# A second layer by 20 block products in place of 21: a 2x4 by 4x3 block algorithm with its sums spread over GpSimd, DMA and VectorE

## The chip, the cores and the metric

The kernel runs on one core of a Trainium2 chip. The metric is the device time of one execution in microseconds (us); the kernel before was run three times. TensorE multiplies matrices and writes PSUM (8 banks of 128 partitions x 512 float32), ScalarE and VectorE read and write PSUM and SBUF, GpSimd works on SBUF, and DMA moves data; each engine works through its own list of instructions in order and waits on semaphores. In the profile PE is TensorE, PEld its weight loads, DVE VectorE, ACT ScalarE, POOL GpSimd, and SP the engine that issues most of the DMA transfers.

## The reference

A causal convolution with 7 taps per head, and on its result a layer pair with a hard swish between, all in float32:

```python
x_unf = x_pad[:, idx, :].reshape(B, S, K, H, group)     # B, S, D = 8, 4096, 192; K = 7, H = 8
x = np.einsum('hk,bskhg->bshg', softmax(weight), x_unf).reshape(B * S, D)
h = x @ w_in                                             # 192 -> 2048
g = h * np.clip(h + 3.0, 0.0, 6.0) / 6.0
out = g @ w_out                                          # 2048 -> 192
```

## The kernel before

The 32768 tokens are worked through in 32 blocks of 1024 tokens. A block has two halves of 512 tokens, numbered k, and a stage each for the two layers. In the first stage (`h_phase`, unchanged) the first layer is computed into PSUM by a Strassen scheme, and `relu` (ScalarE) and `gate` (VectorE) make `g` from it, in four units of dff (the 2048 wide dimension); the second stage multiplies `g` by `w_out`. VectorE also convolves the tokens of the next block during the second stage: seven taps over 128x1536 elements, the first with one tensor as input, the other six with two.

```python
N, P = 512, 128                        # tokens of a half, partitions
g = cst.tile([P, NP, 2, G, N], F32)    # 8 chunks of dff, 2 halves of dff, 2 halves of tokens
def tap(part, k, t):                   # one tap of the convolution
    if k == 0:
        nc.vector.tensor_scalar(out=to, in0=x[...], scalar1=c, scalar2=None, op0=ALU.mult)
    else:
        nc.vector.scalar_tensor_tensor(out=to, in0=x[...], scalar=c, in1=to,
                                       op0=ALU.mult, op1=ALU.add)
def swap(part):                        # the other half's rows beside one's own, by two DMAs
    nc.sync.dma_start(out=y[D2:P, to], in_=y[0:D2, part])
    nc.sync.dma_start(out=y[0:D2, to], in_=y[D2:P, part])
def gate(out, r6, h):                  # h in PSUM, r6 and out in SBUF
    nc.vector.scalar_tensor_tensor(out=out, in0=r6, scalar=1.0, in1=h, op0=ALU.min, op1=ALU.mult)
```

Second stage before: Strassen's seven products of 2x2 blocks. A product is 512 tokens x 1024 of dff x 96 results, so 3 x 8 matmuls of a 128x32 weight tile with 512 tokens; four such tiles lie side by side in the array and run together (`side_by_side`). Of the sums of `g`, two are on GpSimd, unit by unit as `g` appears (`h_phase` calls them), and two on VectorE in the second stage. Each product is drained from PSUM to SBUF by a copy or an addition.

```python
def g_sums(engine, which, slots, width):
    forms = {1: (S1, A21, A22, ALU.add), 3: (S3, A11, A21, ALU.subtract),
             2: (S2, S1, A11, ALU.subtract), 4: (S4, A12, S2, ALU.subtract)}
    ...
            engine.tensor_tensor(out=o[:, r], in0=a[:, r], in1=b[:, r], op=op)
# h_phase, after each unit u > 0:
    g_sums(nc.gpsimd, (1, 3), range(2 * u - 2, 2 * u), 2)     # two of 128x1024

def out_strassen(i, conv):
    for u in conv:                     # the seven taps for block i + 1
        u()
    b, bank = three(1, 2, 0)           # product 1 and a third of product 2: 32 matmuls
    nc.scalar.copy(out=p1[:], in_=bank[m]); piece(p2, 0, bank, NQ); give(b)
    g_sums(nc.vector, (2,), every, 4)  # two of 128x2048
    b, bank = three(4, 2, 1)
    ...
    swap(slice(0, K3))
    b, bank = by_quarters(2, 2)
    ...
    g_sums(nc.vector, (4,), every, 4)
    ...                                # products 7, 6, 3, additions, three stores
    return [lambda: store(i, u3, 1, 1)]    # the fourth store: in the next h_phase

def out_last(i):                       # block 31: the last products in two halves of 256 tokens
    ...
```

The sums of weights are made once, on GpSimd, at the start: four of 128x768 for `w_out`, then four of 128x512 for `w_in` (`w_in_t`). Block 0 is multiplied without such sums (`out_direct`).

Of the kernel before, what the change touches and what calls it, by code (L numbers as in the profile page):

```python
# [16 lines left out]
def kernel(  # L17
# [7 lines left out]
):  # L25

# [96 lines left out]
    w_out = cst.tile([P, NP, 8, DH], F32, name="w_out")  # L123
    B11, B12, B21, B22, T1, T2, T3, T4 = range(8)
# [84 lines left out]
    def w_out_unit(j):  # L209
        dst = w_out[:, j, B11 : B22 + 1].rearrange("p b d -> p (b d)")  # L210
        return Rounding(lambda: load_w_out(j), dst)

    def w_sums():

        def sub(out, x, y):
            nc.gpsimd.tensor_tensor(out=out, in0=x, in1=y, op=ALU.subtract)

        for o, x, y in ((T1, B12, B11), (T3, B22, B12), (T2, B22, T1), (T4, T2, B21)):
            sub(w_out[:, :, o], w_out[:, :, x], w_out[:, :, y])
        b11, b12, b21, b22 = (w_in[:, c::2, s] for s in range(2) for c in range(2))  # L220
        t1, t2, t3, t4 = (w_in_t[:, j] for j in range(4))
        for o, x, y in ((t1, b12, b11), (t3, b22, b12), (t2, b22, t1), (t4, b21, t2)):
            sub(o, x, y)
# [63 lines left out]

    g = cst.tile([P, NP, 2, G, N], F32, name="g")
    g4 = g[:].rearrange("p c h k n -> p c (h k) n")
    A11, A21, A12, A22 = (g4[:, :, j] for j in range(4))  # L290
    S2, S3, S4 = A11, A21, A12
# [123 lines left out]
    def h_phase(left):  # L415
        work = {(u, k): Unit(u, k) for u in range(UNITS) for k in range(2)}
        for u, plan in enumerate(PLANS):
            for step in plan:
                if step == "X":
                    while left:  # L420
                        left.pop(0)()
                    continue
                op = step[1:].rstrip("'+")
                at = u + (step[-1] == "+") - (step[-1] == "'")
                if at < UNITS:
                    work[at, "LU".index(step[0])].run(op)
            if u:
                g_sums(nc.gpsimd, (1, 3), range(2 * u - 2, 2 * u), 2)
# [4 lines left out]
    def mm(bank, j, x, w, q, ps_, first, last, tokens=slice(0, N)):  # L433
# [4 lines left out]
                out=bank[j * QS : (j + 1) * QS, tokens], lhsT=w_out[:, p, w, cols],  # L438
                rhs=x[:, p, tokens],
# [13 lines left out]
    def store_rows(i, k, q, xt, j, dma=nc.sync, tokens=slice(0, N)):  # L453

        t0 = i * TB + k * N
        dma.dma_start(
            out=out[t0 + tokens.start : t0 + tokens.stop, q * QS : (q + 1) * QS].rearrange("(t r) d -> r t d", r=QS),
            in_=xt[j * QS : (j + 1) * QS, tokens].rearrange("r (t d) -> r t d", d=QS),
# [29 lines left out]
    def g_sums(engine, which, slots, width):  # L488

        forms = {  # L490
            1: (S1, A21, A22, ALU.add), 3: (S3, A11, A21, ALU.subtract),
            2: (S2, S1, A11, ALU.subtract), 4: (S4, A12, S2, ALU.subtract),
        }
        for n in which:
            o, a, b, op = forms[n]
            for p in slots[::width]:
                r = slice(p, p + width)
                engine.tensor_tensor(out=o[:, r], in0=a[:, r], in1=b[:, r], op=op)  # L498


    prod = {
        1: (A11, B11), 2: (A12, B21), 3: (S4, B22), 4: (A22, T4),
        5: (None, T1), 6: (S2, T2), 7: (S3, T3),
    }

    def product(bank, j, n, q, ks=every, **tokens):
        x, w = prod[n]
        return mm(bank, j, S1 if n == 5 else x, w, q, ks, True, True, **tokens)

    def four(*parts):  # L510

        b = take()
        bank = psum[:, b]
        side_by_side(*[product(bank, j, n, q) for j, (n, q) in enumerate(parts)])
        return b, bank

    def three(n, n4, q4):
        return four(*[(n, q) for q in range(NQ)], (n4, q4))

    def by_quarters(n, q):  # L520

        b = take()
        bank = psum[:, b]
        w = NP // 4
        side_by_side(
            *[product(bank, j, n, q, range(j * w, (j + 1) * w)) for j in range(4)]
        )
        return b, bank

    def rows(q):  # L530
        return slice(q * QS, (q + 1) * QS)

    def piece(dst, q, src, j):
        nc.scalar.copy(out=dst[rows(q)], in_=src[rows(j)])  # L534

    def pieces(dst, q, src):
        piece(dst, q, src, 0)
        for j in range(1, 4):
            add(dst[rows(q)], dst[rows(q)], src[rows(j)])
# [4 lines left out]
    def store(i, c, k, half_, qs=range(NQ), queues=(nc.sync,), tokens=slice(0, N)):  # L544

        xt = ot.tile([P, N], F32, name="xt")
        r = slice(qs[0] * QS, (qs[-1] + 1) * QS)
        nc.vector.transpose(out=xt[r, tokens], in_=c[r, tokens])  # L548
        for q in qs:
            store_rows(i, k, half_ * NQ + q, xt, q, queues[q % len(queues)], tokens)  # L550

    def sums_tiles():
        return (cs.tile([DH, N], F32, name=f"c{k}") for k in range(6))

    m = slice(0, DH)

    def out_last(i):

        both = nc.sync, nc.scalar
        p1, p2, p4, p5, u2, u3 = sums_tiles()  # L560
        b, bank = three(1, 2, 0)
        nc.scalar.copy(out=p1[:], in_=bank[m])
        piece(p2, 0, bank, NQ)
        give(b)
        g_sums(nc.vector, (2,), every, 4)
        b, bank = four((2, 1), (2, 2), (4, 0), (4, 1))
        for dst, q, j in ((p2, 1, 0), (p2, 2, 1), (p4, 0, 2), (p4, 1, 3)):
            piece(dst, q, bank, j)
        give(b)
        g_sums(nc.vector, (4,), every, 4)  # L570
        add(p2[:], p1[:], p2[:])
        store(i, p2, 0, 0)
        b7, bank7 = three(7, 5, 0)
        piece(p5, 0, bank7, NQ)
        b, bank = three(6, 5, 1)
        piece(p5, 1, bank, NQ)
        add(u2[:], p1[:], bank[m])
        give(b)
        add(u3[:], u2[:], bank7[m])
        give(b7)  # L580
        two = slice(0, 2 * QS)
        add(p4[two], u3[two], p4[two], ALU.subtract)
        store(i, p4, 1, 0, range(2))
        b, bank = by_quarters(5, 2)
        pieces(p5, 2, bank)
        give(b)
        add(u2[:], u2[:], p5[:])
        add(p5[:], u3[:], p5[:])
        store(i, p5, 1, 1)
        for t in range(0, N, N // 2):  # L590
            b = take()
            bank = psum[:, b]
            ts = slice(t, t + N // 2)
            side_by_side(*[
                product(bank, j, n, q, tokens=ts)
                for j, (n, q) in enumerate([(3, 0), (3, 1), (3, 2), (4, 2)])
            ])
            add(u2[:, ts], u2[:, ts], bank[m, ts])
            store(i, u2, 0, 1, queues=both, tokens=ts)
            add(u3[rows(2), ts], u3[rows(2), ts], bank[rows(NQ), ts], ALU.subtract)  # L600
            store(i, u3, 1, 0, range(2, 3), queues=both[::-1], tokens=ts)
            give(b)

    def out_strassen(i, conv):
        p1, p2, p4, p5, u2, u3 = sums_tiles()
        for u in conv:
            u()
        b, bank = three(1, 2, 0)
        nc.scalar.copy(out=p1[:], in_=bank[m])  # L609
        piece(p2, 0, bank, NQ)  # L610
        give(b)
        g_sums(nc.vector, (2,), every, 4)
        b, bank = three(4, 2, 1)
        nc.scalar.copy(out=p4[:], in_=bank[m])  # L614
        piece(p2, 1, bank, NQ)
        give(b)
        swap(slice(0, K3))
        b, bank = by_quarters(2, 2)
        pieces(p2, 2, bank)
        give(b)  # L620
        g_sums(nc.vector, (4,), every, 4)
        add(p2[:], p1[:], p2[:])
        store(i, p2, 0, 0)
        b7, bank7 = three(7, 5, 0)
        piece(p5, 0, bank7, NQ)
        y_sums()
        b, bank = three(6, 5, 1)
        piece(p5, 1, bank, NQ)
        add(u2[:], p1[:], bank[m])
        give(b)  # L630
        add(u3[:], u2[:], bank7[m])
        give(b7)
        add(p4[:], u3[:], p4[:], ALU.subtract)
        store(i, p4, 1, 0)
        b, bank = three(3, 5, 2)
        piece(p5, 2, bank, NQ)
        add(u2[:], u2[:], bank[m])
        give(b)
        add(u2[:], u2[:], p5[:])
        store(i, u2, 0, 1)  # L640
        add(u3[:], u3[:], p5[:])
        return [lambda: store(i, u3, 1, 1)]
# [18 lines left out]
    with tc.manual_schedule():  # L661
# [124 lines left out]
        S1 = ss.tile([P, NP, N], F32, name="s1")[:]  # L786
        left = []
        for i in range(1, NB):
            h_phase(left)
            if i + 1 < NB:  # L790
                left = out_strassen(i, conv_units(i + 1, [slice(0, K3)]))
            else:
                out_last(i)
            if i + 2 < NB:
                x_tiles[i + 2] = load_x(i + 2)

# [32 lines left out]
```

## Time and profile before

| | |
|---|---|
| time, median of 3 (lowest to highest) | 2410.32 us (2410.22 to 2411.18) |
| span of the profiled execution | 2408.5 us, 40221 instructions |
| granted TensorE clock | 1.000 |
| second stage, one steady block | 36.19 us |
| first stage, one steady block | 38.08 us |

Reading: the page's part 1 gives each engine's busy time as a share of the span; part 4 follows the chain of work that ended last back from the end; the groups give every kind of instruction with its count, its mean duration and the idle time before it; the timeline lists instructions by start and duration, with neighbours of one kind merged (x6 is six of them, the duration is that of all six). A group's mean can mix instructions that ran alone with ones that had to wait while running, so the timeline of one block is read beside it. The program's matmul of float32 appears as two records.

### The profile page before, as it was taken

To read this page: it belongs to the slowest core of one execution; us is meant where nothing else is said; L and a number is where in the kernel's file an instruction comes from. 1 tells how busy PE (TensorE), PEld (TensorE's weight loads), DVE (VectorE), ACT (ScalarE), POOL (GpSimd) and SP (SyncE) were. 2 spreads that over 40 slices of the span, in tenths; PEclk is the share of its full clock that TensorE was granted. 3 is DMA by queue.
4 is the path that set the end of the run, shared out by engine and by line. 5 is a ranking of instruction groups with operands and counts; after the bars stand their busy time and mean duration, and the time that the engine had idled before them with its cause. 6 is when DMAs were issued, how large, how long until landed. Compare 5 with 4: busy or idle time off the path is not lost.

```text
span 2408.5 us, 40221 instructions
## 1 busy us (share of the span) xinstructions
PE 2400.5 (100%) x16536; PEld 1019.8 (42%) x16536; DVE 2089.4 (87%) x2533; ACT 1078.4 (45%) x1828; POOL 672.2 (28%) x280
## 2 busy tenths in 40 slices
PE   9999999999999999999999999999999999999999
PEld 5434444334444344443444434444344444344443
DVE  8788888988888888898888898888898888888896
ACT  7234553345543355433454334553345543355433
POOL 2423321233221333122332223322233312333122
PEclk9999999999999999999999999999999999999999
DMA  5211122101222011221112211122201122111210
GB/s 145 40 26 29 27 40 40 39 19 25 39 41 40 19 36 27 40 41 22 33 27 40 41 33 22 27 40 40 40 18 31 34 40 41 21 34 27 40 27 14
DMA packets 227400, 84.65 MB, mean 35 GB/s; under 512 B 205520, under 2 KB 210640, under 8 KB 227216
## 3 DMA queue, kind: packets, MB, share of 16 engines
q1 hardware_dynamic: 225880, 81.56, 17.2%
q8 instruction: 129, 2.11, 0.4%
q10 hardware_dynamic: 1240, 0.27, 0.1%
q14 instruction: 55, 0.45, 0.1%
q0 software_dynamic: 96, 0.26, 0.0%
HBM read 31.72 MB, written 25.17 MB: 24 GB/s over the span
## 4 chain that ended last, share of the span: by engine, by line
PE 99%; DVE 1%; DMA 0%; issue 0%; ACTq 0%; ACT 0%; DVEq 0%
PE psum L311 51%; PE psum L437 48%; DVE c L542 0%; DMA x<-in_x_dram 0%; DVE y L263 0%; DMA out_dram<-xt 0%; DVE xt L548 0%; DVE top L178 0%; ACTq L92 0%; PE psum L676 0%; DVE scale L174 0%; DVE y L259 0%; ACT c L534 0%; DVE scale L195 0%; DVEq L548 0%
## 5 line engine op out<-in xcount | busy, mean ns | idle before, releaser
L437 PE MATMUL psum<-g,w_out 128*32 128x512 f32 (+1 forms) x9376 | 1163.7, 590 | 0.0
L311 PE MATMUL psum<-y,w_in 64*128 64x512 f32 x3664 | 885.2, 591 | 0.6 <-POOL w_in L203 0.3
L498 POOL TENSOR_TENSOR s<-g 128x1024 f32<-128x1024 f32 x124 | 293.6, 2367 | 1644.5 <-DVE g L321 1644.5
L317 ACT ACTIVATE r<-psum,half 128x512 f32<-128x512 f32 x1024 | 642.1, 689 | 241.0 <-PE psum L311 233.9
L437 PEld LDWEIGHTS psum<-g,w_out 128*32 128x32 f32 x9376 | 339.5, 110 | 810.1 <-issue 765.7
L321 DVE SCALAR_TENSOR_TENSOR g<-r,psum 128x512 f32<-128x512 f32 x1024 | 641.6, 681 | 4.9 <-ACT r L317 1.9
L437 PE MATMUL psum<-s,w_out 128*32 128x512 f32 x1488 | 638.5, 592 | 0.0
L311 PEld LDWEIGHTS psum<-y,w_in 64*128 64x128 f32 x3664 | 437.1, 187 | 369.6 <-issue 290.6
L311 PE MATMUL psum<-y,w_in_t 64*128 64x512 f32 x1984 | 524.8, 592 | 0.0
L403 DVE TENSOR_TENSOR psum<-psum,p 128x512 f32<-128x512 f32 x496 | 324.6, 694 | 195.7 <-PE psum L311 186.8
L263 DVE SCALAR_TENSOR_TENSOR y<-x,c_sb,y 128x1536 f32<-128x1536 f32 (+1 forms) x206 | 414.3, 2018 | 6.6
L534 ACT COPY c<-psum 32x512 f32<-32x512 f32 x188 | 108.9, 579 | 600.5 <-PE psum L437 593.5
L498 POOL TENSOR_TENSOR g<-g 128x1024 f32<-128x1024 f32 x124 | 338.5, 2730 | 9.7
L311 PEld LDWEIGHTS psum<-y,w_in_t 64*128 64x128 f32 x1984 | 248.8, 186 | 192.9 <-issue 123.5
L542 DVE TENSOR_TENSOR c<-c,psum 32x512 f32<-32x512 f32 (+2 forms) x189 | 128.4, 679 | 81.2 <-ACT c L534 75.9
L396 ACT COPY psum<-psum 128x512 f32<-128x512 f32 x248 | 138.8, 571 | 72.4 <-PE psum L311 57.6
L437 PEld LDWEIGHTS psum<-s,w_out 128*32 128x32 f32 x1488 | 162.4, 110 | 1.2 <-issue 1.2
L399 ACT COPY p<-psum 128x512 f32<-128x512 f32 x248 | 133.2, 590 | 40.4 <-PE psum L311 39.5
L498 DVE TENSOR_TENSOR g<-s,g 128x2048 f32<-128x2048 f32 x62 | 139.3, 2286 | 3.9 <-POOL g L498 2.3
L498 DVE TENSOR_TENSOR g<-g 128x2048 f32<-128x2048 f32 x62 | 139.4, 2289 | 2.0 <-PE psum L437 1.0
L609 ACT COPY c<-psum 96x512 f32<-96x512 f32 x30 | 17.5, 582 | 174.6 <-PE psum L437 174.6
L614 ACT COPY c<-psum 96x512 f32<-96x512 f32 x30 | 17.5, 583 | 170.0 <-PE psum L437 170.0
(48 smaller groups left out, 438.3 us busy)
## 6 DMA issues: line engine op xcount, KB each, us to landing
out_dram<-xt SPq DMA_DIRECT2D x380, 64.0 KB, 2.0
y<-y SPq DMA_DIRECT2D x62, 384.0 KB, 4.9
x<-in_x_dram SPq DMA_DIRECT2D x55, 388.5 KB, 5.8
stage<-in_moe_w_in_dram SPq DMA_DIRECT2D x16, 192.0 KB, 4.5
stage<-in_moe_w_out_dram SPq DMA_DIRECT2D x8, 384.0 KB, 5.6
x<-in_x_dram SPq DMA_DIRECT2D x7, 384.0 KB
y<-y SPq DMA_DIRECT2D x6, 128.0 KB, 2.3
x<-in_x_dram SPq DMA_DIRECT2D x2, 128.0 KB, 4.5
```

The costliest lines, as they stand in the source:

```text
L263: nc.vector.scalar_tensor_tensor(out=to, in0=x[:, part, k + t : k + t + W], scalar=c, in1=to, op0=ALU.mult, op1=ALU.add,)
L311: nc.tensor.matmul(out=psum[:, b], lhsT=w[r], rhs=y[r, third_of_y], start=start, stop=stop, skip_group_check=onto,)
L317: nc.scalar.activation(r6, h, ACT.Relu, bias=half[:], scale=1.0 / 6.0)
L321: nc.vector.scalar_tensor_tensor(out=out, in0=r6, scalar=1.0, in1=h, op0=ALU.min, op1=ALU.mult)
L396: nc.scalar.copy(out=psum[:, bank["b"]], in_=psum[:, bank["a"]])
L399: nc.scalar.copy(out=self.p5[:], in_=psum[:, bank["e"]])
L403: nc.vector.tensor_tensor(out=psum[:, to], in0=psum[:, bank["b"]], in1=self.p5[:], op=ALU.add)
L437: lambda p=p: nc.tensor.matmul(out=bank[j * QS : (j + 1) * QS, tokens], lhsT=w_out[:, p, w, cols], rhs=x[:, p, tokens], start=(first and p ...
L498: engine.tensor_tensor(out=o[:, r], in0=a[:, r], in1=b[:, r], op=op)
L534: nc.scalar.copy(out=dst[rows(q)], in_=src[rows(j)])
L542: nc.vector.tensor_tensor(out=out, in0=x, in1=y, op=op)
L609: nc.scalar.copy(out=p1[:], in_=bank[m])
```

## The change

The second layer of blocks 1 to 31 is computed by another exact block algorithm: `g` as 2x4 blocks (two halves of tokens, four quarters of dff) times `w_out` as 4x3 blocks (four quarters of dff, three thirds of the 192 results) in 20 products, where the plain way takes 24. It is for fewer matmuls: a product is now 512 tokens x 512 of dff x 64 results, 4 x 2 matmuls of the same 128x32 tile, and 20 of them are 160 matmuls where Strassen's seven were 168. It needs more sums:

- 22 sums and 3 negations of 128x256 blocks of `w_out`, once (`w_sums`);
- five sums per unit of `g` on GpSimd, 128x512 each (`EARLY`), in place of two of 128x1024; place n is `g[k, quarter]` for n < 8 (n = 4 k + quarter) and `extra[n - 8]` for 8 to 10;
- per block five sums of 128x2048 on VectorE and three by DMA that adds to its target (`sum` in `STEPS`), two transfers of 128x1024 elements each;
- the sums of results: a finished half bank of PSUM is copied out by ScalarE (`copy`), put into another half bank as the start of a later product's accumulation (`seed`), or added by VectorE (`join`, `two`).

The taps of the convolution (`conv`) are no longer issued ahead of everything, but between the steps.

```diff
+    EARLY = [                            # GpSimd, per unit, in h_phase
+        (8, 3, 7, '+'), (3, 2, 3, '+'), (9, 2, 8, '+'), (10, 1, 0, '+'), (10, 10, 8, '-'),
+    ]
             if u:
-                g_sums(nc.gpsimd, (1, 3), range(2 * u - 2, 2 * u), 2)
+                for to, a, b, op in EARLY:
+                    g_sum(nc.gpsimd, to, a, b, op, u - 1)
+    STEPS = [          # mm: (place of g, product, node, half bank, starts it)
+        ('conv',), ('mm', (6, 9, 56, 0, 1), (0, 0, 7, 1, 1)), ('conv',),
+        ('mm', (4, 6, 56, 0, 0), (2, 3, 7, 1, 0)), ('sum', 6, 6, 9, '+'),
+        ('mm', (9, 13, 49, 0, 1), (5, 8, 32, 1, 1)), ('sum', 2, 5, 6, '-'), ('copy', 7, (0, 0)),
+        ('seed', 42, 0, (0, 0), 1), ('seed', 45, 1, (0, 0), 1), ('conv',),
+        ('mm', (3, 5, 54, 0, 1), (4, 7, 32, 1, 0)), ('sum', 'dma', 5, 4), ('sum', 9, 7, 10, '+'),
+        ('copy', 49, (0, 0)), ('seed', 9, 0, (0, 0), 1), ('join', 56, (0, 1), None, (0, 0), 1),
+        ('mm', (7, 10, 9, 0, 0), (9, 4, 45, 1, 0)), ('conv',), ('seed', 48, 1, (0, 1), -1),
+        ('copy', 54, (0, 0)), ('sum', 'dma', 3, 2), ('seed', 4, 0, (0, 0), 1), ('conv',),
+        ('seed', 50, 1, (0, 0), 1), ('mm', (1, 2, 4, 0, 0), (2, 18, 50, 1, 0)), ('conv',),
+        ('copy', 45, (0, 0)), ('copy', 9, (1, 0)), ('seed', 41, 0, (0, 0), -1),
+        ('two', 8, (2, 0), (0, 1), (1, 0), -1), ('seed', 1, 1, (1, 0), 1), ('sum', 'dma', 5, 10),
+        ('conv',), ('mm', (10, 12, 41, 0, 0), (6, 15, 48, 1, 0)), ('copy', 50, (1, 0)),
+        ('sum', 9, 9, 3, '+'), ('seed', 18, 0, (1, 0), 1),
+        ('mm', (3, 16, 18, 0, 0), (8, 11, 1, 1, 0)), ('join', 32, (2, 1), None, (1, 0), -1),
+        ('copy', 41, (1, 0)), ('sum', 1, 1, 2, '+'), ('copy', 48, (0, 1)),
+        ('seed', 40, 1, (1, 0), 1), ('join', 32, (2, 1), (2, 1), (0, 1), 1),
+        ('mm', (9, 17, 42, 0, 0), (5, 14, 40, 1, 0)), ('ysums',), ('copy', 18, (1, 1)),
+        ('seed', 2, 1, (1, 1), 1), ('join', 1, (3, 0), None, (1, 0), 1),
+        ('mm', (0, 1, 4, 0, 0), (1, 19, 2, 1, 0)), ('two', 16, (3, 1), (0, 1), (1, 1), -1),
+        ('out', 3, (1, 16)), ...       # three more joins, a store, two joins
+        ('out', 2, (2, 4)),            # the last store: in the next h_phase
+    ]
+            if op == "mm":             # two products, 16 matmuls, four side by side
+                ...
+                for u in range(UNITS):
+                    for place, n, node, k, first in args:
+                        for e in range(2):
+                            nc.tensor.matmul(
+                                out=psum[col : col + QS, nodes.at[node][0]],
+                                lhsT=w[:, u, e * QS : (e + 1) * QS], rhs=g_place(place)[:, u],
+                                start=bool(first and u == 0), stop=(u == UNITS - 1),
+                                tile_position=(0, col), skip_group_check=True)
+            elif op == "sum":
+                if args[0] == "dma":
+                    for u in range(0, UNITS, 2):
+                        us = slice(u, u + 2)
+                        nc.gpsimd.dma_start(out=g_place(args[1])[:, us],
+                            in_=g_place(args[2])[:, us], accum_op=ALU.add)
+                else:
+                    g_sum(nc.vector, *args)
```

Block 31 has no convolution to do and otherwise takes the same steps.

## The prediction

> **What bounds the kernel now.** I read the chain of waits first, then one steady block in the timeline. The chain that ended last is TensorE from end to end, alternating two stages:
>
> ```profile
> 1029.46 36.19 PE psum L437 x336
> 1065.64 38.08 PE psum L311 x174
> ```
>
> 36.19 us for 336 records is 0.1077 us a record: TensorE never stops. 168 matmuls (two records each) are 42 groups of four, 0.862 us a group. So fewer matmuls shorten the span, as long as nothing makes TensorE wait. Who is closest to making it wait is read from the busy times of the two stages (columns: us, then busy us and count of PE, PEld, DVE, ACT, POOL):
>
> ```profile
> 1029.39:1065.58 36.19, 36.19 (x339) 10.82 (x337) 34.19 (x28) 5.34 (x10) 6.33 (x3) 1.00 0.15 31
> 1065.58:1103.65 38.07, 38.07 (x180) 20.35 (x176) 30.98 (x50) 27.80 (x47) 14.04 (x6) 1.00 0.19 36
> ```
>
> VectorE has 34.19 of 36.19 us in the second stage: 2 us free there, and the change adds to it. What it does at the start of that stage:
>
> ```profile
> 1028.90 2.60 DVE L321 SCALAR_TENSOR_TENSOR g<-r,psum 128x512 f32<-128x512 f32 x4
> 1031.41 1.81 DVE L259 TENSOR_SCALAR y<-x,c_sb 128x1536 f32<-128x1536 f32 x1
> 1033.25 5.66 DVE L263 SCALAR_TENSOR_TENSOR y<-x,c_sb,y 128x1536 f32<-128x1536 f32 x2
> 1038.95 5.53 DVE L263 SCALAR_TENSOR_TENSOR y<-x,c_sb,y 128x1536 f32<-128x1536 f32 x3
> 1046.25 4.49 DVE L498 TENSOR_TENSOR g<-s,g 128x2048 f32<-128x2048 f32 x2
> ```
>
> (The third and fourth lines are from narrow windows.) The last gate ends 2.0 us after TensorE began the stage at 1029.39. Then, the same tap costs 1.84 us in one line (5.53/3) and 2.83 in the other (5.66/2). GpSimd shows why:
>
> ```profile
> 1031.04 2.40 POOL L498 TENSOR_TENSOR s<-g 128x1024 f32<-128x1024 f32 x1 [1.51 <-DVE g L321]
> 1033.52 3.78 POOL L498 TENSOR_TENSOR g<-g 128x1024 f32<-128x1024 f32 x1
> ```
>
> The sum beside the first tap (one input tensor) takes its usual 2.40 us and slows nothing. The next, beside taps with two input tensors in SBUF, takes 3.78, and the two taps lose 5.66 - 2 x 1.84 = 1.98 us. They take turns, they do not overlap. At the start of the program it shows larger: four weight sums and the taps for block 1,
>
> ```profile
> 67.14 11.75 POOL L216 TENSOR_TENSOR w_out<-w_out 128x768 f32<-128x768 f32 x4
> 67.73 18.29 DVE L263 SCALAR_TENSOR_TENSOR y<-x,c_sb,y 128x1536 f32<-128x1536 f32 x6
> ```
>
> where six taps take 18.29 in place of 6 x 1.84 = 11.0, so 7.2 us lost to four GpSimd sums.
>
> **What the Trainium skill says.** "SBUF — State Buffer", section "Who interferes with whom": a VectorE instruction with two SBUF inputs contends with a GpSimd instruction that reads SBUF, and the port pair is an exclusive lock for a whole instruction. The trace agrees (3.78 against 2.40; 1.98 us lost). "DMA: Bandwidth & Descriptors", section "SWDGE vs HWDGE vs iDMA": accumulation in a DMA is issued from GpSimd, which writes its descriptors in software; section "Anatomy of one DMA — SWDGE (gpsimd) path": about 2.0 us plus bytes/436e9 for a transfer. For 512 KB that gives an estimate of 3.2 us; nothing in the run before accumulates, so no trace here shows it. "TensorEngine Tiling (Array Packing)", section "When to Use Tiling": 32 weight columns allow four tiles side by side; the trace agrees (a record lasts 592 ns, a new one ends every 108).
>
> **The change part by part.**
>
> TensorE: 160 matmuls are 40 groups, 40 x 0.862 = 34.46 us, so 1.73 us less in each of 31 blocks: 53 us at best, a time near 2357. A step of two products (`mm`) is 16 matmuls, 3.45 us; without waits the ten steps start at 0, 3.45, 6.9, 10.3, 13.8 us and so on. I count all times from the stage's start.
>
> GpSimd: sums of 384 elements take 1.01 us at the program's start, of 1024 take 2.365; a line through both gives 1.28 us for 512. Per unit 5 x 1.28 plus gaps of 0.08 (from the timeline) = 6.8 us in place of 4.8. In the first stage a unit takes 9.45 us, so it fits there, beside gates that have one input in SBUF. But unit 2's last four sums wait for its last gate (end 1099.44 in the block before, 4.2 us ahead of the stage): they end at -4.2 + 4 x 1.36 = 1.3 us. Unit 3's five follow: the first two by about 4.0, under the one-input tap; the last three meet VectorE's two-input work.
>
> VectorE to the first place where TensorE needs it. The fifth `mm` reads place 9 after `sum 9 = 7 + 10`. In VectorE's order there stand before it: tap 1 (1.81), tap 2 (1.84), sum 6 (2.25, half of 4.49), sum 2 (2.25), tap 3 (1.84), and the sum itself (2.25): 12.24 us. From the last gate at 2.0 that ends at 14.3, already 0.5 late. Taking turns with three GpSimd sums of 1.28 adds 3.84: 18.1 us. The order of the turns does not matter, since sum 6 needs the third GpSimd sum and sum 9 the fifth. So TensorE waits at its fifth step from 13.8 to 18.1: 4.3 us.
>
> After that, with T = 18.1: VectorE's join, taps 4 to 6, `two`, tap 7, sum 9, join come to 0.68 + 5.52 + 0.68 + 1.84 + 2.25 + 0.68 = 11.65; three ScalarE copies of 0.58 then fill node 40 by T + 13.5. The ninth step wants it at T + 13.8. Close, no wait. `swap` is issued at about T + 8.8, and in block 0 the sums of y came 5.7 us after the last tap:
>
> ```profile
> 91.73 0.69 DVE L284 TENSOR_TENSOR y<-y 128x512 f32<-128x512 f32 x1 [5.72 <-DMA y<-y]
> ```
>
> which is T + 14.4, where VectorE is then anyway (T + 14.6). VectorE finishes its joins about 2.7 us after TensorE's end of stage; before it was 3.4 (1068.97 against 1065.58) with no wait in the first stage. So the first stage stays 38.08.
>
> The second stage then lasts T + 6 x 3.45 = 18.1 + 20.7 = 38.8 us, 2.6 more than 36.19. Over 30 blocks: +78 us. Block 31 has no taps; there the fifth step waits about 1 us at most, so it gains some 0.7. At the start, GpSimd's 22 weight sums (about 0.75 each) meet the six taps for block 1 and end near 95 us, `w_in_t` near 103, where block 1's first stage starts at 99.8 and needs the first of them at once and the last later: 0 to 3 us. The end (two joins, a transposition, four stores) is as long as before, 6 us. DMA: three sums of 1 MB in two transfers each. With the estimate of 3.2 us per transfer they land inside 8 us each and nothing waits, but the margin is small: the first is issued near 14, the second right behind, their results are wanted at 27 (VectorE) and 32 (TensorE, after the third sum, which waits for the first). I put 5 us of the total on occasional lateness.
>
> Sum: 2410 + 78 - 1 + 2 + 5 = 2494.
>
> **The rivals.**
>
> (a) The sums are hidden and the matmuls count: 2357 to 2365. For it: over a block VectorE has 65.17 us of 74.26, the change adds about 2.1 (one more 128x2048 sum 2.25, one more 64x512 addition, one transposition less), so on average there is room for it. Against: the wait arises at one place, 14 us into the stage, and TensorE's order is fixed; later room does not give it back.
>
> (b) The lock costs less than whole turns, or GpSimd is ahead when the taps begin. Then T is 14.3 to 16 and the stage 35.0 to 36.7: a time of 2375 to 2425, about the same as before. For it: only the two cases above show the lock, with larger sums. Against: both show nearly the sum of the two durations.
>
> (c) The accumulating DMA is slow. It reads its target as well as its source. A plain `swap` of 2 x 384 KB lands in 4.9 us; if accumulating halves that rate, 1 MB takes about 10 us, the second sum lands after 34 in place of 27 and VectorE and TensorE stand still for some 7 us more: 2600 to 2700. Against: the changed order seems made for windows of about 10 us.
>
> **Range and chances.** The wait at the fifth step carries the prediction. 1 us of it is worth 30 us of time. If T is 1.5 us early the time is 2450, if DMA adds 2.5 us a block it is 2570. Range 2420 to 2575, predicted 2490. To be 2% faster (below 2362) nearly no wait may arise in any block, and VectorE's own 12.24 us speak against that even without the lock: 0.05. Within 2% (up to 2458), T up to about 17 us: 0.25. Slower: 0.70.
>
> **What would show each step.** In the chain, second stages of about 38.8 us, no longer 36.19, with first stages at 38.08. In the waits, TensorE (or its weight load) waiting for VectorE's 128x2048 sum into `extra`, some 4 us in each of 30 blocks, and none in block 31 above 1 us. Taps 2 and 3 and the sums 6 and 2 longer than 1.84 and 2.25 next to GpSimd sums of over 1.28. A mean of 1.28 us for a GpSimd sum in the first stage. It would be wrong if GpSimd's sums end before the taps, if TensorE waits for a DMA (rival c), for ScalarE's seeds (a chain of dependent copies longer than 0.58 each), or if VectorE's lateness reaches into the first stage.

## The result and the profile after

The changed kernel takes 2672.36 us (median of 4, 2666.78 to 2679.48) where the one before takes 2410.40: a ratio of 1.1088 (95% interval 1.1061 to 1.1115). The prediction said 2490, with 2420 to 2575 as range.

The chain of waits of the kernel after, the rows of two neighbouring first stages (start, us):

```profile
596.98 38.08 PE psum L338 x174
678.83 38.08 PE psum L338 x174
```

The first stage still lasts 38.08 us. Between the end of one and the start of the next, 635.06 to 678.83, lie 43.77 us of second stage in place of 36.19. Over all blocks: first stages start at 182.84 and, 29 blocks later, at 2585.32, so 82.84 us a block and 44.8 for the second stage. The busy times of the two stages (us, then PE, PEld, DVE, ACT, POOL, the granted clock, the DMA share, GB/s):

```profile
596.98:635.06 38.08, 38.08 (x180) 19.25 (x184) 30.77 (x51) 27.20 (x47) 17.84 (x15) 1.00 0.22 38
635.06:678.83 43.77, 38.26 (x322) 10.81 (x320) 37.89 (x31) 13.45 (x23) 17.94 (x12) 0.96 0.53 95
```

TensorE now stands for 5.5 us, its clock is 0.96, and DMA has gone from 0.15 to 0.53. VectorE at the start of that stage (TensorE began it at 634.94):

```profile
636.97 1.81 DVE L290 TENSOR_SCALAR y<-x,c_sb 128x1536 f32<-128x1536 f32 x1
638.81 2.62 DVE L294 SCALAR_TENSOR_TENSOR y<-x,c_sb,y 128x1536 f32<-128x1536 f32 x1
641.35 3.37 DVE L568 TENSOR_TENSOR g<-g,extra 128x2048 f32<-128x2048 f32 x1
644.81 3.18 DVE L568 TENSOR_TENSOR g<-g 128x2048 f32<-128x2048 f32 x1
647.92 1.80 DVE L294 SCALAR_TENSOR_TENSOR y<-x,c_sb,y 128x1536 f32<-128x1536 f32 x1
649.65 2.28 DVE L568 TENSOR_TENSOR extra<-g,extra 128x2048 f32<-128x2048 f32 x1
```

and GpSimd beside it:

```profile
638.53 1.28 POOL L568 TENSOR_TENSOR extra<-g,extra 128x512 f32<-128x512 f32 x1
639.76 2.80 POOL L568 TENSOR_TENSOR extra<-g 128x512 f32<-128x512 f32 x1
642.64 3.21 POOL L568 TENSOR_TENSOR extra<-extra 128x512 f32<-128x512 f32 x1
```

These are the predicted turns: the tap and two sums take 2.62, 3.37 and 3.18 us where they take 1.8, 2.28 and 2.28 alone, and two GpSimd sums 2.80 and 3.21 in place of 1.28. The sum into place 9 ends at 651.93, 17.0 us into the stage (predicted 18.1). But TensorE's waits are more than this one (in brackets the idle time of the engine before the line, and what ended it):

```profile
650.28 1.05 PE L621 MATMUL psum<-g,w_t 128*32 128x512 f32 x4 [1.40 <-ACT psum L645]
652.70 1.06 PE L621 MATMUL psum<-extra,w_t 128*32 128x512 f32 x2 [1.36 <-DVE parts L574]
...
658.44 4.24 PE L621 MATMUL psum<-g,w_t 128*32 128x512 f32 x32 [0.74 <-ACT psum L645]
664.02 0.62 PE L621 MATMUL psum<-extra,w_t 128*32 128x512 f32 x2 [1.34 <-ACT psum L647]
...
675.19 3.64 PE L621 MATMUL psum<-g,w_t 128*32 128x512 f32 x32 [0.67 <-DVE parts L574]
```

Ahead of the steps 5, 6 and 7 (a step is one `mm`) it waits for ScalarE's seeds, and at 652.70 not for the sum but for the `join` behind it. ScalarE in turn waits for TensorE:

```profile
649.03 0.58 ACT L639 COPY parts<-psum 64x512 f32<-64x512 f32 x1 [5.15 <-PE psum L621]
...
657.80 1.19 ACT L645 COPY psum<-parts 64x512 f32<-64x512 f32 x2 [4.01 <-PE psum L621]
662.17 1.17 ACT L639 COPY parts<-psum 64x512 f32<-64x512 f32 x2 [3.17 <-PE psum L621]
```

The first of these copies node 49 (a node is a result in its half bank), which step 3 finished 10.3 us into the stage. It starts at 14.1, when step 4 ends. Step 4 does not touch node 49, but it adds to node 32, which lies in the other half of the same PSUM bank. The part of the page on DMA (KB of each transfer, median us from issue to landing):

```profile
g<-g POOLq DMA_DIRECT2D x124, 512.0 KB, 8.8
g<-extra POOLq DMA_DIRECT2D x62, 512.0 KB, 11.3
...
y<-y SPq DMA_DIRECT2D x62, 384.0 KB, 5.6
```

An adding transfer lands after 8.8 or 11.3 us, where the prediction estimated 3.2.

So there are three suspects: the turns (predicted), the shared banks, the adding DMA.

### The profile page after: what moved, and what is told of

The parts are those of the page before. It is cut to its first block, busy times and chain, and to the rows that moved or that the text cites. A ratio compares the mean times of both kernels' runs of the same rounds, so it can differ in the third digit from the quotient of the medians.

```text
span 2669.4 us, 40470 instructions
## 1 busy us (share of the span) xinstructions
PE 2458.6 (92%) x15976; PEld 981.8 (37%) x15976; DVE 2194.1 (82%) x2558; ACT 1312.1 (49%) x2233; POOL 1158.3 (43%) x856
## 3 DMA queue, kind: packets, MB, share of 16 engines
q0 software_dynamic: 50688, 97.79, 21.8%
## 4 chain that ended last, share of the span: by engine, by line
PE 64%; DVE 20%; issue 7%; DMA 5%; ACT 3%; SPq 0%; DVEq 0%; ACTq 0%
PE psum L338 46%; PE psum L621 16%; DVE g L568 5%; DMA y<-y 5%; DVE y L294 3%; DVE extra L568 3%; DVE parts L574 3%; DVE y L315 2%; DVE y L290 2%; PE psum L465 2%; DVE g L348 1%; ACT parts L639 1%; ACT r L344 1%; ACT psum L645 1%; SPq L307 0%
## 5 line engine op out<-in xcount | busy, mean ns | idle before, releaser
L621 PE MATMUL psum<-g,w_t 128*32 128x512 f32 x7440 | 1156.3, 607 | 119.1 <-ACT psum L645 66.4
L568 POOL TENSOR_TENSOR extra<-g 128x512 f32<-128x512 f32 x248 | 361.8, 1459 | 970.0 <-DVE g L348 970.0
L621 PE MATMUL psum<-extra,w_t 128*32 128x512 f32 x2480 | 578.3, 619 | 83.4 <-ACT psum L647 41.7
L621 PEld LDWEIGHTS psum<-g,w_t 128*32 128x32 f32 x7440 | 313.8, 112 | 623.3 <-issue 351.3
L639 ACT COPY parts<-psum 64x512 f32<-64x512 f32 x310 | 179.8, 580 | 692.8 <-PE psum L621 451.6
L568 POOL TENSOR_TENSOR g<-g 128x512 f32<-128x512 f32 x124 | 158.1, 1275 | 289.6 <-DVE g L348 287.2
L568 POOL TENSOR_TENSOR extra<-extra 128x512 f32<-128x512 f32 x124 | 218.4, 1762 | 9.7
L645 ACT COPY psum<-parts 64x512 f32<-64x512 f32 x279 | 163.2, 585 | 117.6 <-PE psum L621 110.8
L631 POOL DMA_DIRECT2D g<-g x124 | 152.2, 1950 | 86.0 <-DVE g L568 65.1
L568 POOL TENSOR_TENSOR extra<-g,extra 128x512 f32<-128x512 f32 x124 | 158.5, 1278 | 0.0
## 6 DMA issues: line engine op xcount, KB each, us to landing
g<-extra POOLq DMA_DIRECT2D x62, 512.0 KB, 11.3
```

What stands on the lines that cost most here:

```text
L568: engine.tensor_tensor(out=g_place(to)[:, u], in0=g_place(a)[:, u], in1=g_place(b)[:, u], op={"+": ALU.add, "-": ALU.subtract}[op],)
L621: nc.tensor.matmul(out=psum[col : col + QS, nodes.at[node][0]], lhsT=w[:, u, e * QS : (e + 1) * QS], rhs=g_place(place)[:, u], start=bool( ...
L631: nc.gpsimd.dma_start(out=g_place(args[1])[:, us], in_=g_place(args[2])[:, us], accum_op=ALU.add,)
L639: nc.scalar.copy(out=tile_half(*at), in_=nodes(node))
L645: nc.scalar.copy(out=nodes(node), in_=tile_half(*at))
```

## The experiments

All are edits of the changed kernel. Each of the suspects has an edit that takes it away; with all combinations of the three, and a few more, they can be told apart.

**A bank for each result.**

```diff
-            b = next((b for b, u in self.used.items() if k not in u), None)
-            if b is None:
-                b = take()
-                self.used[b] = set()
+            b = take()
+            self.used[b] = set()
```

> Every half-bank result gets a PSUM bank of its own (at most 7 are alive at a time, and there are 8 banks); nothing else changes. Bank theory: copies, seeds and joins wait for matmuls into the other half of the same bank, so TensorE's waits for ScalarE go away; what is left is the late sum into place 9 (16.9 us into the stage in the block I read, plus six steps of 3.45 us): a second stage of 37.7 to 39.2 us in place of a mean of 44.8, a time of 2450 to 2520. Turns theory (VectorE and GpSimd taking turns at SBUF, as predicted, is the whole loss) and DMA theory (the accumulating transfers land too late): no change, 2650 to 2690.

Measured: 2644.59 us, ratio to before 1.0969 (1.0950 to 1.0987). The waits on the other half are gone: in a stage that began at 632.20, node 49 is copied at the end of step 3,

```profile
642.79 0.58 ACT L637 COPY parts<-psum 64x512 f32<-64x512 f32 x1 [1.64 <-PE psum L619]
```

but the time falls by only 28 us. TensorE now waits inside step 9 for the last adding transfer, which lands 37.1 us into the stage, where the prediction wanted it at 32:

```profile
669.34 0.94 PE L619 MATMUL psum<-g,w_t 128*32 128x512 f32 x2 [2.22 <-DMA g<-extra]
```

The bank theory by itself missed by far, and no change at all is not what was found either: the banks were in the way, and behind them stood something as slow.

**Without the three sums by DMA** (left out).

```diff
-                    for u in range(0, UNITS, 2):
+                    for u in range(0, 0, 2):
```

> The changed kernel without its three sums by DMA (part of the computation is left out). DMA theory: TensorE and VectorE no longer wait for transfers of 8.8 to 11.3 us, so some 100 us or more less, below 2570. Bank theory and turns theory: the transfers landed before their readers needed them, 2640 to 2680.

Measured: 2642.11 us (ratio 1.0961, 1.0939 to 1.0983), 30 us less, in the range of the bank and turns theories. Read alone, this run would say that DMA hardly matters.

**Without the last three GpSimd sums of the last unit** (left out, blocks 2 to 31; `late` is true there).

```diff
-                for to, a, b, op in EARLY:
+                for to, a, b, op in EARLY[: 2 if late and u == UNITS else 5]:
```

> The changed kernel without the last three of GpSimd's five sums for the last unit of a block, blocks 2 to 31 (part of the computation is left out): the sums that meet VectorE's two-input work. Turns theory: the second tap and the sums 6 and 2 fall from 2.62, 3.37 and 3.18 us to 1.84, 2.25 and 2.25, and the sum into place 9 ends 2.8 us earlier. If it alone held TensorE, 80 to 90 us less (2580 to 2595); with the bank theory beside it, TensorE still waits at the same step for ScalarE's seed, so 40 to 60 us less (2610 to 2635). If the turns are no part of the loss: 2660 to 2680.

Measured: 2629.77 us (ratio 1.0910, 1.0888 to 1.0931), 43 us less, in the range for turns and banks side by side.

**Banks and GpSimd sums together.** Both edits.

> Both at once: a bank for each result, and without the last three GpSimd sums of the last unit (part of the computation is left out). Bank and turns together being all of the loss: the fifth step waits 0.3 us, a second stage of 34.8 us and a time near 2370. If the accumulating DMA stands behind them as the next limit (its three sums last some 18 us from 11 to 13 us into the stage, and the ninth step wants the last at 28 to 29 us): a stage of 36 to 38 us and 2410 to 2470, with TensorE waiting for DMA at the ninth step.

Measured: 2566.09 us (ratio 1.0645, 1.0624 to 1.0667): 106 us less, more than the 28 and 43 of the two alone, and still far above both expectations. The chain of waits in one of its blocks shows what is left (start, us):

```profile
640.35 10.79 DMA y<-y
...
651.23 1.91 DVE y L315 x3
```

`swap`, a plain copy by another queue, takes 10.8 us here beside the adding transfers, with the DMA engines busy for 96% of this stretch; VectorE's sums of y wait for it. TensorE also waits for the last adding transfer, 93 us in total at its weight loads.

**All three taken away** (GpSimd's and DMA's sums left out).

> All three suspects taken away at once: a bank for each result, without the last three GpSimd sums of the last unit, and without the three sums by DMA (parts of the computation are left out in the last two). If banks, turns and DMA together are the whole loss, the second stage is 34.5 to 35.5 us and the time 2360 to 2400. If VectorE's own work (36.5 us of it from 2 us into the stage on) reaches into the first stage besides: 2400 to 2450, with TensorE waiting for VectorE there.

Measured: 2402.18 us (ratio 0.9966, 0.9950 to 0.9982). The waits of the second stage are gone:

```profile
1027.12:1062.32 35.20, 35.20 (x323) 13.88 (x321) 34.49 (x29) 13.46 (x23) 3.51 (x3) 1.00 0.11 25
```

and yet it is 45 us above the 2357 of TensorE's work alone. VectorE, busy for 34.49 of these 35.20 us, comes late into the next first stage, where TensorE now waits for a bank that VectorE has still to drain:

```profile
1064.62 1.55 PE L338 MATMUL psum<-y,w_in_t 64*128 64x512 f32 x5 [0.31 <-DVE parts L575]
```

The chain runs through VectorE from 1027.89 to 1064.57 and through TensorE for the following 36.34 us; a block takes 73.8 us in place of 34.46 + 38.08 = 72.5. The prediction had compared the end of VectorE's joins with the kernel before, 3.4 us after the stage without a wait. But there VectorE's last read of a bank ended 1.4 us after the stage (1067.00 against 1065.58); here the one that TensorE waits for ends 2.3 us after it (1064.57 against 1062.32). From the kernel before:

```profile
1066.32 0.68 DVE L542 TENSOR_TENSOR c<-c,psum 96x512 f32<-96x512 f32 x1 [2.16 <-ACT c L534]
```

Whether the own banks, of which more are in use at the end of a stage, add to this wait was not tested.

**Banks and DMA taken away, the turns left.**

> A bank for each result and no sums by DMA (those three left out); the turns of VectorE and GpSimd remain. This is the world that the prediction described: the sum into place 9 at 16.9 us, then six steps of 3.45 us without a wait. With the prediction's turns alone: a stage of 37.7 us, 2455 to 2470. If TensorE falls to half its clock after the wait, as it did in the changed kernel, 1.5 us more a block: 2500 to 2515.

Measured: 2496.07 us (ratio 1.0356, 1.0326 to 1.0386), between the two ranges. The sum into place 9 ends 17.0 us into the stage, TensorE waits for it, and then runs slowly:

```profile
772.49 0.62 PE L619 MATMUL psum<-extra,w_t 128*32 128x512 f32 x2 [2.27 <-DVE extra L568]
...
774.14 1.07 PE L619 MATMUL psum<-extra,w_t 128*32 128x512 f32 x2
...
776.70 0.68 PE L619 MATMUL psum<-extra,w_t 128*32 128x512 f32 x2
```

The granted clock of this stretch is the number after POOL's busy time:

```profile
772.49:776.20 3.71, 3.71 (x24) 1.06 (x28) 3.64 (x3) 2.28 (x4) 0.00 (x0) 0.63 0.00 0
```

The granted clock falls to half 15 times in the 30 blocks of this run, for 3.4 us each. In the other blocks it does not: at 541.83, after a wait of 2.21 us, TensorE goes on at full speed.

**GpSimd sums and DMA taken away, the banks left.** Both edits on the changed kernel.

> Without the last three GpSimd sums of the last unit and without the sums by DMA (both left out), half banks shared as in the changed kernel. What shared banks cost by themselves: the fifth step waits for a copy and a seed after the fourth (1.4 us), the sixth to tenth some 0.7, 1.9 and 0.8 us more: a stage of 39 to 40 us and 2500 to 2530. If banks matter only beside the other two, 2360 to 2420.

Measured: 2536.70 us (ratio 1.0525, 1.0494 to 1.0555). A little above the range; shared banks cost much by themselves.

**A filled wait.** Own banks, no sums by DMA, and ahead of step 5:

```diff
             if op == "mm":
+                if args[0][1] == 10:
+                    b = take()
+                    for _ in range(3):
+                        nc.tensor.matmul(out=psum[:, b], lhsT=w_in_t[:, 0, 0],
+                            rhs=g_place(0)[:, 0], start=True, stop=True)
+                    give(b)
```

> As the run with own banks and no sums by DMA, but three matmuls of 128x128 with 512 tokens, whose result nobody reads, stand ahead of the fifth step and fill 2.6 us of TensorE's wait there. Theory that the wait itself brings TensorE to half its clock: the slow matmuls after it are gone and the time falls by up to 45 us (1.5 us in each of 30 blocks). Theory that the slow clock has another cause, or costs nothing beyond the wait: no change within 10 us.

Measured: 2483.75 us (ratio 1.0305, 1.0275 to 1.0335). The mean clock goes from 0.989 to 0.999 and the slow matmuls are gone, so it was the wait that slowed the clock. Only 12 us come of it, where up to 45 were expected: TensorE then waits for VectorE at the start of the next first stage, as in the run above with everything taken away. A block then takes 76.6 us; the first stages, in the chain from that wait on:

```profile
254.54 36.34 PE psum L338 x166
331.11 36.34 PE psum L338 x166
```

**Copies in place of additions.** Own banks and without the three GpSimd sums, and the six transfers do not add (the addition is left out).

```diff
                             out=g_place(args[1])[:, us], in_=g_place(args[2])[:, us],
-                            accum_op=ALU.add,
```

> As the run with own banks and without the last three GpSimd sums of the last unit (2566 us), but the six DMA transfers of a block copy in place of adding (part of the computation is left out: the addition). If adding is what makes them slow, since the target is read too: transfers land in about half the time, swap is no longer held up, 2402 to 2450. If 3 MB between SBUF and SBUF in this stretch are too much for the DMA engines in any case: 2540 to 2570.

Measured: 2400.28 us (ratio 0.9957, 0.9941 to 0.9973), the same as with no transfers at all. From its page:

```profile
g<-g POOLq DMA_DIRECT2D x124, 512.0 KB, 4.1
g<-extra POOLq DMA_DIRECT2D x62, 512.0 KB, 5.4
...
y<-y SPq DMA_DIRECT2D x62, 384.0 KB, 5.0
```

The same bytes land in 4.1 and 5.4 us (8.5 and 13.9 in the run that differs only in the addition), and `swap` in 5.0 (8.9).

**Taps 2 and 3 later, the whole computation.** Own banks, and the second and third `('conv',)` moved behind the step `('mm', (7, 10, 9, 0, 0), (9, 4, 45, 1, 0))`.

> The whole computation, a bank for each result, and taps 2 and 3 moved behind the fifth step, so that VectorE makes the sums 6, 2 and 9 first. Turns theory: the sum into place 9 ends near 14.1 us in place of 16.9, and the first DMA can start 1.7 us earlier. With DMA as the next limit: 2 to 3 us less a block than with own banks alone (2645), 2555 to 2585. If VectorE's whole list is the limit and not one place in it: 2630 to 2650.

Measured: 2652.10 us (ratio 1.1004, 1.0986 to 1.1023), nothing gained over own banks alone and outside both ranges. Its chain shows DMA, not VectorE's order, in charge:

```profile
643.68 12.31 DMA g<-g
...
656.11 2.29 DVE extra L568
```

**The same order, without the sums by DMA** (left out).

> The same order of taps and own banks, without the sums by DMA (left out). If the place of the taps made the late sum: as without the GpSimd sums, 2400 to 2430 in place of 2496. If VectorE's list as a whole, 36.5 us and 2.8 us of turns from 2 us into the stage on, is the limit wherever the taps stand: 2460 to 2500.

Measured: 2492.18 us (ratio 1.0340, 1.0319 to 1.0361), 4 us from the run with the taps in their old place and inside the second range. In a stage that began at 677.26 the sum into place 9 ends 13.7 us into it, not 17.0:

```profile
688.67 2.28 DVE L568 TENSOR_TENSOR extra<-g,extra 128x2048 f32<-128x2048 f32 x1
```

TensorE does not wait for it any more, and nearly nothing is gained: it waits for seeds later in the stage and for VectorE at the start of the next first stage. VectorE's list as a whole limits, wherever the taps stand.

**Own banks, all GpSimd sums, copies in place of additions** (the addition is left out).

> A bank for each result, all of GpSimd's sums, and the six DMA transfers of a block as copies instead of additions (the addition is left out). This has the turns, and transfers about as short as the prediction assumed (3.2 us), without shared banks. If the prediction erred only in the banks and in the length of the adding transfers, this is its 2490: as without the transfers (2496), within 10 us. If the transfers cost something even when short, 2510 or more.

Measured: 2497.86 us (ratio 1.0362, 1.0345 to 1.0380), 2 us from the run without transfers.

All combinations in one table (us; "left" is what remains in place, "banks" are the shared ones):

| left | time | | left | time |
|---|---|---|---|---|
| banks, turns, DMA | 2672 | | banks | 2537 |
| turns, DMA | 2645 | | turns | 2496 |
| banks, DMA | 2630 | | DMA | 2566 |
| banks, turns | 2642 | | none | 2402 |

Read from the right, each of the three costs much: banks 135, turns 94, DMA 164 us over "none". Read from the left, taking one away brings 28, 43 or 30 us. They limit the same stretch side by side; the next one takes over. Read from the world of the prediction, turns alone (2496), either of the other two is enough to leave its range: shared banks add 146 us, adding DMA 149, both together 176.

## Why the prediction was wrong

**TensorE's saving.** Right as a count: 40 groups of four, and 35.2 us for a second stage when nothing is in the way. But it was never the bound: even with everything taken away a block takes 73.8 us, with VectorE's list in the chain.

**The turns.** Right in kind, too large in size. The sum ended at 17.0 us, not 18.1: each of the three GpSimd sums cost VectorE less than its own 1.28 us, 0.8, 1.1 and 0.9 us on the tap and the two sums, 2.8 in place of 3.84. The trace of the kernel before already showed this. The prediction put the 7.2 us lost by six taps at the start of the program down to four weight sums, but the last two taps ran beside sums of `w_in_t`, 128x512 like the later ones, and lost 0.88 us each:

```profile
80.54 2.72 DVE L263 SCALAR_TENSOR_TENSOR y<-x,c_sb,y 128x1536 f32<-128x1536 f32 x1
81.60 2.80 POOL L216 TENSOR_TENSOR w_in_t<-w_in 128x512 f32<-128x512 f32 x1
```

A term left out was the clock: in the block shown above, six steps after the wait took 22.4 us (772.49 to 794.91), not 20.7. "The Trainium skill", page "TensorE: Matmul & The Clock Gate", section "Part 1: The HAM clock gate", has the clock fall to half after an idle window of about 3.4 us; here it fell after a wait of 2.27 us, though not after each wait of that length, and the measurement decides.

The run with own banks and short transfers is the world that the prediction described, and it takes 2497.86 where 2490 was predicted. In part that is luck. The two errors above have opposite signs, and the wait at the fifth step did not carry the time as the prediction said ("1 us of it is worth 30 us of time"): the sum 3.3 us earlier brought 4 us, the filled wait 12 us. VectorE's lateness at the start of the first stage, which the prediction had excluded, makes a block of 76.6 us by itself, close to the predicted 38.8 + 38.08 = 76.9.

**DMA: the step that failed.** "With the estimate of 3.2 us per transfer they land inside 8 us each and nothing waits", and 5 us for the total. An adding transfer is not a copy of its size: it took 8.5 and 13.9 us where the copy took 4.1 and 5.4. Beside the turns it adds 149 us (2645 against 2496), which alone leads out of the predicted range; with the other two suspects gone it costs 164 us, partly through `swap`, which took 8.9 us beside it and 5.0 beside copies. Rival (c) named this mechanism and its time, 2600 to 2700, holds the result. But the rival was not the explanation as it stood: in the changed kernel, leaving out the transfers gains 30 us only, since the shared banks stand beside them.

**The banks: a step that was not there.** The prediction let each copy start when its own product was finished, and found it "Close, no wait". In the program a copy, seed or join also waits for the matmuls of the other half of its bank, so ScalarE and TensorE alternate. That own banks lift these waits is shown (node 49 above); the cost by itself is 135 us, and 146 us beside the turns (2642 against 2496), which alone leads out of the range too. Waits of TensorE for ScalarE's seeds and for a DMA both stood in the prediction's list of what would show it wrong. The skill's page "PSUM — Partial Sum Buffer", section "PSUM bank collisions raise a hardware error", says that different quadrants (groups of 32 partitions) of one bank may be used at once and that guarding by bank is the simple version. No run here tried guarding by quadrant, so it stays open whether this program could do without the waits while sharing banks.

**The first stage and the start.** 38.08 us after as before, as predicted. The weight sums ended at 98.6 us, ahead of the 99.8 where they are first needed, so there was no loss (0 to 3 predicted).

**Rival (a)** fell as argued, but for more than was argued: not just one place 14 us into the stage but the whole of VectorE's list was too long. Moving the taps, with the turns left, changed 4 us. Rival (b), a T of 14.3 to 16 us, is not met either: T was 17.0.

What stays open is how the 270 us between the changed kernel and the run with all three taken away divide among the three. The table says that they overlap, not that each has a share. None of the runs that do the whole computation came near the kernel before.

## What to carry to other kernels

When work moves from the engine that bounds a kernel to three others, look for limits that stand side by side: taking one away then shows little, and only the combinations show what each is worth. A transfer that adds must be counted by what the DMA engines do for it (here about twice the packets of a copy), and by what else runs on them. And results that share a bank, or any unit by which the program sets its waits, are tied to each other's producers.

## What the runs showed of the hardware

- A DMA from SBUF to SBUF that adds: 50688 packets and 22.8% of the DMA engines over the span (the run with own banks and without the GpSimd sums), against 26880 packets and 11.0% in the run that differs only in that the same bytes are copied. The issue of one takes 1.20 us of GpSimd in place of 0.72.
- TensorE at half its clock for 3.4 us after a wait of 2.3 us in half of the blocks (matmul records of 1.07 us in place of 0.60), and in none when other matmuls filled the wait.
- GpSimd and VectorE with two SBUF inputs take turns also in pieces of 1.28 us: VectorE lost 2.8 us to three sums that take 3.84 alone.
